# An opening in another order: the first batch's fold ahead of weight conversion, its norm on ScalarE, and weights converted by shifts and xors

## The chip, the cores and the metric

The kernel runs on one core of one Trainium2 chip. The metric is the device time of one execution in microseconds (us); lower is better. Before the change the median of 3 runs was 461.93 us (461.61 to 462.76).

A core has five engines that run their own instruction queues, each strictly in order, and wait for each other by semaphores: TensorE (PE in the profile; its weight loads are PEld), VectorE (DVE), ScalarE (ACT), GpSimd (POOL) and SyncE (SP), which here issues all the DMA transfers.

## The reference

Four batches, 1088 tokens, model width 128. Three blocks follow each other.

- Attention with a feature map instead of a softmax. For 4 heads of 32 columns, every query and key becomes the 64 products of two 8-wide projections (with S1 and S2, float64 inputs). keys give `kv = sum k_p v` and `z = sum k_p`, queries give `num / (den + 1e-6)`.
- A Fourier block: `u = x + real(fft over tokens and columns of x)`, then a layer norm `un = (u - mu) / sqrt(var + 1e-6)`, then `u + relu(un @ w_ch1) @ w_ch2` with 512 hidden columns.
- A gated block: `h = relu(x @ w_in)` with 1024 columns, halves u and v; v is normalized, mixed over tokens by a 1088 x 1088 matrix `w_spatial` with a bias, multiplied with u and projected by `w_out`.

The weights w_ch1, w_ch2, w_in and w_out reach the chip as float64 bit patterns, two 32-bit words for each number. The kernel must turn them into fp32 itself.

## The kernel before, in words

**Precision.** A large matrix product is made of three matmuls in a reduced fp32 type: high half by high half, high by low, low by high. So each operand is split: ScalarE copies it with rounding (the high half), and VectorE or GpSimd subtracts that from the original (the low half, `sub`, line 114, whose trace rows all stand under that line).

**Weight conversion.** `weight(n, k)` (line 331) takes one block of 256 columns, calls `from_f64`, lets ScalarE make the high half (line 333) and GpSimd the low half. There are ten blocks: two each of w1 and w2, four of wi (0 and 1 for u, 2 and 3 for v), two of wo. `from_f64` (line 305) splits the upper word into exponent, mantissa and sign (lines 312, 315, 316 on VectorE), shifts the exponent's range on ScalarE with two Relus (313, 314), turns the lower word into a fraction on ScalarE (311), puts mantissa and exponent together on VectorE (317, 318) and multiplies both on GpSimd (320). Its scratch tiles have two buffers each.

**Stages of one batch.** `keys(b)` and `queries(b)` make the features: three matmuls per group (line 353, `abp`), a ScalarE copy (355, two buffers `ab`), the products on VectorE (359, `pp`), then for keys 72 small matmuls (376, `kv`), for queries transposes (397, `qps`), ScalarE copies (402) and the numerator (408, `nm`), which VectorE divides into `ub[b]` (416 to 418). `fourier_seq(b)` folds the tokens and columns by the symmetry of the cosines and sines: sums and differences on VectorE (438 `eo`, 442 `fe`, 447 `l_`, 451 `lrb`) and small copies on GpSimd, then the transform's matmuls (462, `dft`). Its first pair of matmuls needs a piece of the second pass of the fold. `fourier_feat(b)` transforms the columns (491, 504) and VectorE adds the result to `ub[b]` (499, 506).

`channel(b)` (line 165) is the norm, the Fourier block's two matrix products and the v half of the gated block. Its nine token tiles come in three chunks of three. `stats` computes mean and variance of tiles on VectorE (179, 180) and 1/sigma by a ScalarE square root and four VectorE steps (`rstd`); before the change one call covers all nine tiles. For each chunk: `un`, the normalized tile, on VectorE (195); transposes (199 `t1`, 206 `t2`); the halves of the transposed tile (202 on ScalarE, `sub` on VectorE, `unl`); four hidden blocks (`ch1`, lines 214 to 216; their halves at 219 on ScalarE and 220 on VectorE, `hl`) and `ch2` (225 to 227); the sum and its halves (241 to 243), the v matmuls (254 to 256), statistics and norm of v and its halves. For batch 0 the chunk's small matmul results share two PSUM buffers.

`spatial(b)` is the token mixing (604 to 606), gate and output; its splitting of the matrix (`spatial_split`) runs on ScalarE, GpSimd and VectorE.

**Order.** The program text gives the priority: a planner walks through time with its own costs and puts on each engine's queue the ready instruction that comes first in the text; later work fills slots in which earlier work isn't ready. Three tools bend that. `issue_after(ins)` puts the instructions of a block that run on the same engine as `ins` behind it in that engine's queue (order alone, no wait). `keep_in_program_order` pins an instruction behind the one traced before it on its engine. And the hooks of `channel` run a function at a chosen chunk: `hooks[2c]` before the hidden blocks of chunk c, `hooks[2c+1]` before its v matmuls. `warm(n)` issues n matmuls of zeros that nobody reads, 11 at the start, 10 in the fold of batch 0, 20 ahead of channel(0).

The opening in the text before: loads of batch 0, tables, six weight blocks, batch 1, four weight blocks; keys(0), queries(0), weights w1, fourier_seq(0), fourier_feat(0), weights wi 2 and 3, warm(20), channel(0) (with w2 and wo converted at chunk 0, wi 0 and 1 at chunk 2), keys(1), queries(1), loads of batch 2, and the split of the first token mixing matrix. From batch 1 on, channel(b+1) is interleaved with spatial(b).

Of the kernel before, what the change touches and what calls it, by code (L numbers as in the profile page):

```python
# [7 lines left out]
F32 = mybir.dt.float32  # L8
F32R = mybir.dt.float32r
I32 = mybir.dt.int32  # L10
U32 = mybir.dt.uint32
ACTF = mybir.ActivationFunctionType
ALU = mybir.AluOpType
# [52 lines left out]
def fourier_attention_gmlp_kernel(  # L66
# [46 lines left out]
    def sub(eng, lo, x, hi):  # L113
        eng.tensor_tensor(out=lo, in0=x, in1=hi.bitcast(F32), op=ALU.subtract)  # L114
# [50 lines left out]
    def channel(b, pe, psm, tagm, nm, psc, tagc, vn, hooks=(None,) * 7):  # L165
# [9 lines left out]
        def stats(tiles):  # L175
            mv_ = pe.tile([P, len(tiles), 2], F32, tag="mv1", bufs=nb, name="mv1")
            for i, j in enumerate(tiles):
                bst = pe.tile([P, 6], F32, tag="bst", bufs=2, name="bst")
                V.bn_stats(out=bst, in_=u_[:, j, :])
                V.bn_aggr(out=mv_[:, i, :], in_=bst)  # L180
            r_ = rstd(pe, mv_, len(tiles), "l1", nb)
            for i, j in enumerate(tiles):
                mv[j], rs[j] = mv_[:, i, 0:1], r_[:, i, :]

        def hook(i):
            if hooks[i] is not None:
                hooks[i]()

        stats(range(NT))
        for c in range(3):  # L190
            c0, n, full = CH[c]
            tiles = tiles_of(c)
            un = pe.tile([P, 3, DM], F32, tag="un", bufs=nb, name="un")
            for j, i in tiles:
                marks[b, c, "un"] = V.tensor_scalar(out=un[:, i, :], in0=u_[:, j, :], scalar1=mv[j], scalar2=rs[j],
                                op0=ALU.subtract, op1=ALU.mult)
            t1 = mt("t1")
            for j, i in tiles:
                marks[b, c, "t1"] = T.transpose(out=t1[:, 128 * i:128 * i + 128], in_=un[:, i, :], identity=ident if j < 8 else psel)
            unh = pe.tile([P, 384], F32R, tag="unh", bufs=nb, name="unh")  # L200
            unl = pe.tile([P, 384], F32R, tag="unl", bufs=nb, name="unl")
            marks[b, c, "unh"] = A.copy(out=unh[:, 0:n], in_=t1[:, 0:n])
            sub(V, unl[:, 0:n], t1[:, 0:n], unh[:, 0:n])
            t2 = mt("t2")
            for j, i in tiles:
                T.transpose(out=t2[:, 128 * i:128 * i + 128], in_=u_[:, j, :], identity=ident if j < 8 else psel)
            xt = const.tile([P, 384], F32, tag="x2", bufs=3, name="xt")
            A.copy(out=xt[:, 0:n], in_=t2[:, 0:n])
            yield
            c2 = psc.tile([P, 512], F32, tag=tagc, name="c2")  # L210

# [92 lines left out]

    def from_f64(raw, n, out, fast):

        w = raw.rearrange("p (n two) -> p n two", two=2)
        lo_, hi_ = w[:, 0:n, 0], w[:, 0:n, 1]
        tl = lambda nm, dt: pre.tile([P, 256], dt, tag=nm, bufs=2, name=nm)[:, 0:n]
        x, e, s, r = tl("dx", I32), tl("dy", I32), tl("ds", I32), tl("dr", F32)  # L310
        A.activation(out=r, in_=lo_.bitcast(U32), func=ACTF.Copy, scale=2.0 ** -52)
        V.tensor_scalar(out=e, in0=hi_, scalar1=20, scalar2=0x7FF, op0=ALU.logical_shift_right, op1=ALU.bitwise_and)
        A.activation(out=e, in_=e, func=ACTF.Relu, bias=cst[:, 1:2])
        A.activation(out=e, in_=e, func=ACTF.Relu, scale=-1.0, bias=cst[:, 2:3])
        V.tensor_scalar(out=x, in0=hi_, scalar1=0xFFFFF, scalar2=0x100000, op0=ALU.bitwise_and, op1=ALU.bitwise_or)
        V.tensor_scalar(out=s, in0=hi_, scalar1=-2 ** 31, scalar2=0x7F800000, op0=ALU.bitwise_and, op1=ALU.bitwise_xor)
        V.scalar_tensor_tensor(out=r, in0=x, scalar=2.0 ** -20, in1=r, op0=ALU.mult, op1=ALU.add)
        V.scalar_tensor_tensor(out=s, in0=e, scalar=23, in1=s, op0=ALU.logical_shift_left, op1=ALU.bitwise_xor)
        out = r if out is None else out
        (V if fast else G).tensor_tensor(out=out, in0=r, in1=s.bitcast(F32), op=ALU.mult)  # L320
        return out

    wraw = {}
# [7 lines left out]
    def weight(n, k):  # L331
        w_ = from_f64(wraw.pop((n, k)), 256, None, False)
        A.copy(out=wt[n][:, k, 0, :], in_=w_)
        sub(G, wt[n][:, k, 1, :], w_, wt[n][:, k, 0, :])
# [90 lines left out]
    def fourier_seq(b):  # L425
# [10 lines left out]
        for i, op in enumerate((ALU.add, ALU.subtract)):  # L436
# [8 lines left out]
            for par in range(2):  # L445
                o2 = ALU.add if par == i else ALU.subtract
                V.tensor_tensor(out=l_[:, i, par, :, i:64], in0=ev[:, :, 0, i:64], in1=ev[:, :, 1, i:64], op=o2)
                if i == 0:
                    G.tensor_tensor(out=lz[:, :, par, 63:64], in0=eov[:, :, 0, 64:65], in1=eov[:, :, 1, 64:65], op=o2)
                rows = slice(64 * i + 32 * par, 64 * i + 32 * par + 32)  # L450
                V.tensor_tensor(out=lrb[rows, i, par, 1 - i:64 - i], in0=rs_[rows, 1:64], in1=rs_[rows, 127:64:-1], op=op)
                if i == 0:
                    G.tensor_copy(out=lrb[rows, 0, par, 0:1], in_=rs_[rows, 0:1])
                    G.tensor_copy(out=lrb[rows, 1, par, 63:64], in_=rs_[rows, 64:65])
# [86 lines left out]
    load_raw("wsh0", blocks[6:])  # L541
    keys(0)
    queries(0)
    weight("w1", 0)
    weight("w1", 1)
    fourier_seq(0)
    fourier_feat(0)
    weight("wi", 2)
    weight("wi", 3)
    warm(20)  # L550
    def convert(*part):
        def run():
            for n, k in part:
                weight(n, k)

        return run

    for _ in channel(0, pre, psy, "acc", 2, psy, "o", None, [convert(("w2", 0), ("w2", 1), ("wo", 0), ("wo", 1)), None, None, None, convert(("wi", 0), ("wi", 1)), None]):
        pass
    keys(1)  # L560
    queries(1)
    loads(2)
    with tc.issue_after(marks[0, 1, "t1"].ins):
        spatial_split(pre, 0, [G], spatial_load(const, 0, ring))
# [186 lines left out]
```

## Time and profile before

| | |
|---|---|
| median of 3 runs | 461.93 us (461.61 to 462.76) |
| the profiled execution, its own time | 462.66 us |
| its span, first to last instruction | 460.7 us |
| mean granted TensorE clock | 0.984 of full speed |
| busy: PE, DVE, ACT, POOL | 441.3, 276.4, 191.7, 68.4 us |

The rows of the later section are from the profiled execution; times in them are us from the start of its span. Busy times of TensorE are modelled ends of pipelined matmuls, so a busy engine may still run below its peak rate; its granted clock is shown beside it as a share of full speed. An idle time in a row is the engine's own idle time just before the instruction, with what ended it.

### The profile page before, as it was taken

Reading aid. Unit: us, or ns where it says so; the run is one execution under the profiler, and the core shown is the slowest. Engines: PE = TensorE matmul, PEld = TensorE weight load, DVE = VectorE, ACT = ScalarE, POOL = GpSimd, SP = SyncE. Lnnn points to the kernel's source line nnn. Section 1 sums busy time; section 2 is a strip of 40 time slices with the busy share of each in tenths; the row PEclk is TensorE's granted clock in tenths of the full one; section 3 lists DMA queues with packets and bytes.
Section 4 is the critical chain, followed back from the end, with each engine's and each line's share of the span. In section 5 each row is a group of like instructions: output and inputs, shape, how many; then the busy total and the mean of one; then the engine's idle time right before and its main releaser. Section 6 shows DMA issues by size and latency. Waiting matters only on the chain.

```text
span 460.7 us, 7484 instructions
## 1 busy us (share of the span) xinstructions
PE 441.3 (96%) x2893; PEld 405.5 (88%) x2893; DVE 276.4 (60%) x685; ACT 191.7 (42%) x448; POOL 68.4 (15%) x105
## 2 busy tenths in 40 slices
PE   8889699899999999999999999999999999999996
PEld 7766589567879789899999999999999999999995
DVE  5688988987563596789736363883645456222221
ACT  3545596365223154456524243552423335212221
POOL 2154485572110150000000000000000000000000
PEclk9979799999999999999999999999999999999999
DMA  8992132011003100000000000000000000000000
GB/s 254 359 314 97 52 92 83 0 39 34 0 1 93 38 17 1 0 1 20 14 1 0 18 0 1 18 1 14 2 0 18 0 19 1 14 1 17 1 17 16
DMA packets 13007, 19.29 MB, mean 42 GB/s; under 512 B 1446, under 2 KB 11436, under 8 KB 12844
## 3 DMA queue, kind: packets, MB, share of 16 engines
q1 hardware_dynamic: 12972, 18.82, 12.7%
q8 instruction: 23, 0.38, 0.4%
q14 instruction: 12, 0.10, 0.1%
HBM read 16.58 MB, written 2.23 MB: 41 GB/s over the span
## 4 chain that ended last, share of the span: by engine, by line
PE 77%; issue 9%; DVE 9%; ACT 3%; POOL 1%; POOLq 0%; DVEq 0%; ACTq 0%
PE ac L605 12%; PE ac L604 12%; PE ac L606 12%; PE dft L462 3%; PE v_ps L254 2%; PE v_ps L256 2%; PE c L225 2%; PE c L227 2%; PE c L226 2%; PE v_ps L255 2%; PE nm L408 2%; PE ac L612 2%; PE ac L611 1%; PE u_ps L597 1%; PE u_ps L598 1%
## 5 line engine op out<-in xcount | busy, mean ns | idle before, releaser
L606 PE MATMUL ac<-wsh,vlo 128*128 128x384 f32 (+1 forms) x384 | 126.3, 329 | 2.2 <-POOL vlo L114 2.2
L604 PE MATMUL ac<-wsh,vh 128*128 128x384 f32 (+1 forms) x384 | 126.7, 330 | 0.1
L605 PE MATMUL ac<-wsl,vh 128*128 128x384 f32 (+1 forms) x384 | 126.4, 329 | 0.0
L606 PEld LDWEIGHTS ac<-wsh,vlo 128*128 128x128 f32 x384 | 72.0, 188 | 3.3 <-POOL vlo L114 3.1
L605 PEld LDWEIGHTS ac<-wsl,vh 128*128 128x128 f32 x384 | 72.1, 188 | 1.6 <-issue 0.8
L604 PEld LDWEIGHTS ac<-wsh,vh 128*128 128x128 f32 x384 | 72.1, 188 | 1.5 <-ACT vh L270 0.4
L615 DVE TENSOR_TENSOR uh<-ac,uh 128x384 f32<-128x384 f32 (+1 forms) x48 | 25.4, 529 | 57.0 <-PE ac L612 55.2
L601 ACT ACTIVATE uh<-u_ps 128x384 f32<-128x384 f32 (+1 forms) x48 | 22.6, 471 | 48.0 <-PE u_ps L599 45.5
L114 DVE TENSOR_TENSOR gl<-uh,gh 128x384 fp32r<-128x384 f32 (+1 forms) x48 | 26.2, 548 | 12.9 <-ACT gh L616 12.7
L245 POOL CAST xh<-xh 128x64 fp32r<-128x64 f32 x4 | 2.1, 514 | 201.8 <-ACT xh L242 201.8
L359 DVE TENSOR_TENSOR pp<-ab 128x768 f32<-128x768 f32 x23 | 23.7, 1062 | 11.8 <-ACT ab L355 11.4
L261 DVE BATCH_NORM_STATS2 bst<-vn 128x6 f32<-128x512 f32 x27 | 18.6, 693 | 16.7 <-ACT vn L259 16.6
L616 ACT CAST gh<-uh 128x384 fp32r<-128x384 f32 (+1 forms) x48 | 23.5, 492 | 12.2 <-DVE uh L615 11.9
L259 ACT ACTIVATE vn<-v_ps 128x512 f32<-128x512 f32 x27 | 16.0, 598 | 19.1 <-PE v_ps L256 18.6
L241 DVE TENSOR_TENSOR xt<-c,xt 128x384 f32<-128x384 f32 (+1 forms) x12 | 6.4, 534 | 27.7 <-PE c L227 27.7
L408 PE MATMUL nm<-kvz,qp 128*128 128x66 f32 x144 | 17.4, 271 | 0.0
L408 PEld LDWEIGHTS nm<-kvz,qp 128*128 128x128 f32 x144 | 17.2, 192 | 0.1
L282 ACT CAST vh<-vn 128x1024 fp32r<-128x1024 f32 x12 | 12.6, 1047 | 10.3 <-PE ac L605 8.2
L242 ACT CAST xh<-xt 128x384 fp32r<-128x384 f32 (+1 forms) x12 | 6.0, 497 | 26.0 <-DVE xt L241 26.0
L225 PE MATMUL c<-hh,w 128*128 128x384 f32 (+1 forms) x48 | 16.6, 346 | 0.0
L597 PE MATMUL u_ps<-sxh,wi 128*128 128x384 f32 (+1 forms) x48 | 16.3, 339 | 0.3 <-ACT uh L601 0.3
L227 PE MATMUL c<-hl,w 128*128 128x384 f32 (+1 forms) x48 | 16.3, 340 | 0.0
(714 smaller groups left out, 961.6 us busy)
## 6 DMA issues: line engine op xcount, KB each, us to landing
wst<-in_wsp SPq DMA_DIRECT2D x18, 192.0 KB, 2.8
vx<-in_vt SPq DMA_DIRECT2D x12, 198.0 KB, 4.3
kt<-in_kT SPq DMA_DIRECT2D x12, 192.0 KB, 6.2
qt<-in_qT SPq DMA_DIRECT2D x12, 192.0 KB, 4.4
w2st<-in_wsp SPq DMA_DIRECT2D x9, 160.0 KB, 4.1
tr<-in_trig SPq DMA_DIRECT2D x1, 1096.0 KB
wraw<-in_w SPq DMA_DIRECT2D x4, 256.0 KB, 7.7
wraw<-in_win SPq DMA_DIRECT2D x4, 256.0 KB, 5.2
```

What stands on the lines that cost most here:

```text
L114: eng.tensor_tensor(out=lo, in0=x, in1=hi.bitcast(F32), op=ALU.subtract)
L225: mm(out=c2[:, 0:n], lhsT=wpart("w2", 0, 128 * m, 128), rhs=hh[:, 0:n], start=(m == 0), stop=False)
L227: mm(out=c2[:, 0:n], lhsT=wpart("w2", 0, 128 * m, 128), rhs=hl[:, 0:n], start=False, stop=(m == 3))
L359: (G if [b, tag[0], c] in [[3, 'k', 2]] else V).tensor_tensor(out=pp, in0=a_.unsqueeze(3).to_broadcast([P, 12, 8, 8]), in1=b_.unsqueeze(2) ...
L408: mm(out=nm[:, t, 2 * pr:2 * pr + 2, :].rearrange("p h d -> p (h d)"), lhsT=qp[:, pr, 128 * t:128 * t + 128], rhs=z[:, pr, :], start=True, ...
L597: mm(out=h_[:, 0:n], lhsT=wpart("wi", 0, 128 * m, 128), rhs=xh[:, 0:n], start=True, stop=False)
L601: A.activation(out=uh[:, 0:n], in_=h_[:, 0:n], func=ACTF.Relu)
L604: mm(out=ac[:, 0:n], lhsT=vh[:, k, ms], rhs=wsh[c][:, k, :], start=(k == 0), stop=False)
L605: mm(out=ac[:, 0:n], lhsT=vh[:, k, ms], rhs=wsl[c][:, k, :], start=False, stop=False)
L606: mm(out=ac[:, 0:n], lhsT=vl[:, k, ms], rhs=wsh[c][:, k, :], start=False, stop=False)
L615: V.tensor_tensor(out=uh[:, 0:n], in0=ac[:, 0:n], in1=uh[:, 0:n], op=ALU.mult)
L616: A.copy(out=gh[:, 0:n], in_=uh[:, 0:n])
```

## The change

- In `channel`, `stats` is called for tiles 0 to 2 alone when b is 0, and for tiles 3 to 8 behind chunk 0's transposes; for other batches it still covers nine. It computes one more small tile, minus mean times 1/sigma, and `un` becomes a ScalarE instruction with that as bias and 1/sigma as scale, for every batch.
- `from_f64` has other steps: ScalarE takes the absolute value of the upper word read as a float, a maximum and a minimum clamp it (GpSimd for weights, VectorE for the first small matrix), VectorE shifts it left and right, shifts three bits of the lower word in, and puts sign and exponent offset in by xors; the last step is on VectorE for every block.
- The VectorE instructions of w1's conversion, and of w2's (now ahead of channel(0) in place of wi 2 and 3), are queued behind the last fold instruction of batch 0. wi 2 and 3 are converted at chunk 0, wi 0 and 1 at chunk 1, wo at chunk 2.
- The VectorE instructions of keys(1) and queries(1) are queued behind `unl` of chunk 0.

```diff
             r_ = rstd(pe, mv_, len(tiles), "l1", nb)
+            m_ = pe.tile([P, len(tiles), 1], F32, tag="l1m", bufs=nb, name="m_")
+            V.scalar_tensor_tensor(out=m_, in0=mv_[:, :, 0:1], scalar=-1.0, in1=r_, op0=ALU.mult, op1=ALU.mult)
             for i, j in enumerate(tiles):
-                mv[j], rs[j] = mv_[:, i, 0:1], r_[:, i, :]
+                mv[j], rs[j] = m_[:, i, :], r_[:, i, :]
...
-        stats(range(NT))
+        stats(range(3) if b == 0 else range(NT))
...
             for j, i in tiles:
-                marks[b, c, "un"] = V.tensor_scalar(out=un[:, i, :], in0=u_[:, j, :], scalar1=mv[j], scalar2=rs[j],
-                                op0=ALU.subtract, op1=ALU.mult)
+                A.activation(out=un[:, i, :], in_=u_[:, j, :], func=ACTF.Identity, bias=mv[j], scale=rs[j])
...
-            sub(V, unl[:, 0:n], t1[:, 0:n], unh[:, 0:n])
+            marks[b, c, "unl"] = V.tensor_tensor(out=unl[:, 0:n], in0=t1[:, 0:n], in1=unh[:, 0:n].bitcast(F32), op=ALU.subtract)
...
             A.copy(out=xt[:, 0:n], in_=t2[:, 0:n])
+            if b == 0 and c == 0:
+                stats(range(3, NT))
             yield
...
-        x, e, s, r = tl("dx", I32), tl("dy", I32), tl("ds", I32), tl("dr", F32)
-        A.activation(out=r, in_=lo_.bitcast(U32), func=ACTF.Copy, scale=2.0 ** -52)
-        V.tensor_scalar(out=e, in0=hi_, scalar1=20, scalar2=0x7FF, op0=ALU.logical_shift_right, op1=ALU.bitwise_and)
-        A.activation(out=e, in_=e, func=ACTF.Relu, bias=cst[:, 1:2])
-        A.activation(out=e, in_=e, func=ACTF.Relu, scale=-1.0, bias=cst[:, 2:3])
-        V.tensor_scalar(out=x, in0=hi_, scalar1=0xFFFFF, scalar2=0x100000, op0=ALU.bitwise_and, op1=ALU.bitwise_or)
-        V.tensor_scalar(out=s, in0=hi_, scalar1=-2 ** 31, scalar2=0x7F800000, op0=ALU.bitwise_and, op1=ALU.bitwise_xor)
-        V.scalar_tensor_tensor(out=r, in0=x, scalar=2.0 ** -20, in1=r, op0=ALU.mult, op1=ALU.add)
-        V.scalar_tensor_tensor(out=s, in0=e, scalar=23, in1=s, op0=ALU.logical_shift_left, op1=ALU.bitwise_xor)
+        a, s, r = tl("dx", I32), tl("ds", I32), tl("dr", F32)
+        A.activation(out=a.bitcast(F32), in_=hi_.bitcast(F32), func=ACTF.Abs)
+        (V if fast else G).tensor_scalar(out=a.bitcast(F32), in0=a.bitcast(F32), scalar1=2.0 ** -15, scalar2=1.875 * 2.0 ** 16,
+                                         op0=ALU.max, op1=ALU.min)
+        V.tensor_scalar(out=s, in0=hi_, scalar1=-2 ** 31, scalar2=0x40000000, op0=ALU.bitwise_and, op1=ALU.bitwise_xor)
+        V.tensor_scalar(out=a, in0=a, scalar1=4, scalar2=1, op0=ALU.logical_shift_left, op1=ALU.logical_shift_right)
+        V.scalar_tensor_tensor(out=s, in0=lo_, scalar=29, in1=s, op0=ALU.logical_shift_right, op1=ALU.bitwise_xor)
         out = r if out is None else out
-        (V if fast else G).tensor_tensor(out=out, in0=r, in1=s.bitcast(F32), op=ALU.mult)
+        V.tensor_tensor(out=out.bitcast(I32), in0=a, in1=s, op=ALU.bitwise_xor)
...
-                V.tensor_tensor(out=lrb[rows, i, par, 1 - i:64 - i], in0=rs_[rows, 1:64], in1=rs_[rows, 127:64:-1], op=op)
+                marks[b, "fold"] = V.tensor_tensor(out=lrb[rows, i, par, 1 - i:64 - i], in0=rs_[rows, 1:64],
+                                                   in1=rs_[rows, 127:64:-1], op=op)
...
-    weight("w1", 0)
-    weight("w1", 1)
     fourier_seq(0)
+    with tc.issue_after(marks[0, "fold"].ins):
+        weight("w1", 0)
+        weight("w1", 1)
     fourier_feat(0)
-    weight("wi", 2)
-    weight("wi", 3)
+    with tc.issue_after(marks[0, "fold"].ins):
+        weight("w2", 0)
+        weight("w2", 1)
     warm(20)
...
-    for _ in channel(0, ..., [convert(("w2", 0), ("w2", 1), ("wo", 0), ("wo", 1)), None, None, None, convert(("wi", 0), ("wi", 1)), None]):
+    for _ in channel(0, ..., [convert(("wi", 2), ("wi", 3)), None, convert(("wi", 0), ("wi", 1)), None, convert(("wo", 0), ("wo", 1)), None]):
         pass
-    keys(1)
-    queries(1)
+    with tc.issue_after(marks[0, 0, "unl"].ins):
+        keys(1)
+        queries(1)
     loads(2)
```

## Rows read from the trace of the kernel before

**Rows 1.** Stretches: PE, PEld, DVE, ACT, POOL busy us; TensorE clock; DMA share, GB/s.
```profile
20.00:30.00 10.00, 7.34 (x88) 6.63 (x90) 9.90 (x25) 4.83 (x13) 3.85 (x10) 0.99 0.98 314
30.00:40.00 10.00, 10.00 (x66) 5.84 (x64) 7.37 (x21) 4.95 (x14) 6.47 (x7) 0.67 0.76 249
...
50.00:58.00 8.00, 7.12 (x26) 6.08 (x26) 7.22 (x18) 4.46 (x11) 2.78 (x4) 0.57 0.03 10
...
80.00:110.00 30.00, 26.17 (x200) 19.53 (x200) 28.23 (x53) 14.65 (x33) 17.48 (x22) 1.00 0.10 27
...
200.00:400.00 200.00, 200.00 (x1196) 193.98 (x1195) 116.71 (x293) 83.35 (x185) 2.21 (x6) 1.00 0.02 8
```

**Rows 2.** Timeline of TensorE, 28 to 53 us: start, length, line, operation [idle before].
```profile
28.06 3.23 PE L376 MATMUL kv<-vx,pp 128*64 128x33 f32 x72 [2.05 <-DVE pp L359]
...
31.63 1.18 PE L462 MATMUL dft<-tr,l__380 128*64 128x274 f32 x2
...
41.60 4.84 PE L519 MATMUL wp<-a 128*128 128x512 f32 x20
...
50.15 0.42 PE L199 MATMUL t<-prm,un 128*128 128x128 f32 x1 [3.31 <-DVE un L195]
...
52.37 0.69 PE L214 MATMUL h__605<-unh,w 128*128 128x384 f32 x1 [0.74 <-ACT unh L202]
```

**Rows 3.** Timeline of VectorE, 20 to 32 us.
```profile
20.39 0.28 DVE L316 TENSOR_SCALAR ds<-wraw 128x256 int32<-128x256 int32 x1
...
22.20 0.69 DVE L438 TENSOR_TENSOR eo<-ub 128x512 f32<-128x512 f32 x1
...
26.24 0.29 DVE L312 TENSOR_SCALAR dy<-wraw 128x256 int32<-128x256 int32 x1
...
27.05 3.56 DVE L359 TENSOR_TENSOR pp<-ab 128x768 f32<-128x768 f32 x4
...
31.46 0.49 DVE L447 TENSOR_TENSOR l__380<-fe 128x126 f32<-128x126 f32 x2
```

**Rows 4.** Groups by line and form, 0 to 120 us: busy, mean ns | idle before.
```profile
L313 ACT ACTIVATE dy<-dy,cst 128x256 int32<-128x256 int32 x10 | 4.9, 504 | 4.3 <-DVE dy L312 4.3
...
L195 DVE TENSOR_SCALAR un<-ub,mv,r 128x128 f32<-128x128 f32 x9 | 3.3, 434 | 0.0
...
L179 DVE BATCH_NORM_STATS2 bst<-ub 128x6 f32<-128x128 f32 x9 | 2.1, 268 | 0.0
...
L313 ACT ACTIVATE dy<-dy,cst 128x64 int32<-128x64 int32 x1 | 0.3, 348 | 0.0
```

**Rows 5.** The same view: conversion and products.
```profile
L359 DVE TENSOR_TENSOR pp<-ab 128x768 f32<-128x768 f32 x18 | 18.1, 1047 | 5.8 <-ACT ab L355 5.5 <-PE kv L376 0.3
...
L320 POOL TENSOR_TENSOR dr<-dr,ds 128x256 f32<-128x256 f32 x10 | 7.9, 797 | 7.4 <-DVE ds L318 7.3
...
L318 DVE SCALAR_TENSOR_TENSOR ds<-dy,ds 128x256 int32<-128x256 int32 x10 | 5.4, 544 | 1.6 <-ACT dy L314 1.5
...
L312 DVE TENSOR_SCALAR dy<-wraw 128x256 int32<-128x256 int32 x10 | 4.7, 474 | 0.1
L317 DVE SCALAR_TENSOR_TENSOR dr<-dx,dr 128x256 f32<-128x256 int32 x10 | 4.7, 472 | 1.1 <-ACT dr L311 1.1
...
L316 DVE TENSOR_SCALAR ds<-wraw 128x256 int32<-128x256 int32 x10 | 3.6, 358 | 0.0
...
L315 DVE TENSOR_SCALAR dx<-wraw 128x256 int32<-128x256 int32 x10 | 2.8, 276 | 0.0
```

**Rows 6.** Stretch from 52 to 80 us, VectorE alone: busy, clock, DMA.
```profile
52.00:80.00 28.00, 24.19 (x57) 0.91 0.26 72
```

**Rows 7.** Line 451 by its operations: min/median/max ns, first and last start.
```profile
L451 DVE TENSOR_TENSOR lrb<-rs__1229 x4: 203/218/1198, 84.8 to 91.9; 32x63 f32<-32x63 f32 x4
```

**Rows 8.** GpSimd's timeline from 85 us.
```profile
85.01 3.89 POOL L114 TENSOR_TENSOR vlo<-v,vh 128x512 fp32r<-128x512 f32 x3
```

**Rows 9.** Groups, 0 to 120 us: the activation tables' load.
```profile
L511 ACT ACT_TABLE_LOAD x1 | 1.3, 1283 | 0.7 <-PEq L737 0.7
```

More of the change, by code (lines that the diff above doesn't have):

```diff
@@ L556, in convert @@
         return run
-    for _ in channel(0, pre, psy, "acc", 2, psy, "o", None, [convert(("w2", 0), ("w2", 1), ("wo", 0), ("wo", 1)), None, None, None, convert(("wi", 0), ("wi", 1)), None]):
+    for _ in channel(0, pre, psy, "acc", 2, psy, "o", None, [convert(("wi", 2), ("wi", 3)), None, convert(("wi", 0), ("wi", 1)), None, convert(("wo", 0), ("wo", 1)), None]):
         pass
-    keys(1)
-    queries(1)
+    with tc.issue_after(marks[0, 0, "unl"].ins):
+        keys(1)
+        queries(1)
     loads(2)
```

## The prediction

> **What bounds the kernel now.** I read the table of stretches first. From 110 us on TensorE has hardly a gap: 200 of 200 us are busy between 200 and 400, at the full clock [rows 1]. Its work there does not change, so whatever the opening saves reaches the end unless another engine takes it back on the way. The loss lies before 110. TensorE was granted a mean clock of 0.67 between 30 and 40 us and 0.57 between 50 and 58, so parts of these stretches ran at 1.2 GHz; between 80 and 110 it is busy 26.17 of 30 us. In the same table VectorE is nearly full: 9.90 of 10 us (20 to 30) and 28.23 of 30 (80 to 110).
>
> Next TensorE's own timeline, for what it waits on [rows 2]. At 28.06 it has waited 2.05 us for a product of batch 1. It then enters the Fourier matmuls (31.63) with the low clock. After the filler of 20 matmuls (41.60 to 46.4) and four small ones it waits 3.31 us for the first normalized tile, and the first weight matmuls (52.37) fall into the second stretch with a low clock. Both times the clock fell behind a gap of 2 to 3 us.
>
> Last VectorE's timeline for the cause [rows 3]. Attention of batch 0 ends at about 20.4, but the fold (lines 438 to 451), which the Fourier matmuls need, is cut up: conversion from 20.39 to 22.20, again at 26.24, four products of batch 1 at 27.05, and only at 31.46 the last half of the fold.
>
> What can be got back at most: the two gaps, 2.05 + 3.31 = 5.4; the clock between 30 and 40, 10 x (1 - 0.67) = 3.3; between 50 and 58, 8 x (1 - 0.57) = 3.4; in all 12.1, say 12.2 with the 0.1 lost between 20 and 30. The filler's 4.84 us stays, since nothing removes it.
>
> **The change, part by part.**
>
> *Order around the fold.* The VectorE instructions of keys and queries of batch 1 go behind the low half of chunk 0, and those of w1 and w2 behind the fold. From VectorE's rows this takes 1.81 us (20.39 to 22.20), 0.81 (26.24 to 27.05) and some 3.5 (the four products from 27.05) out of the fold's way, with about 0.5 of smaller pieces: 6.6. The Fourier matmuls then start near 25 instead of 31.63. TensorE has batch 1's feature matmuls to fill until then, up to five groups of six before buffers stop it, so I expect no gap and the full clock. From 31.63 to the filler's start behind the second transform (41.60) is 10.0 us [rows 2]. Less the 3.3 of clock, and an estimated 1 of batch 1's transposes and features that lie in between, it is about 5.7; the filler starts near 31 instead of 41.6.
>
> *Statistics of three tiles instead of nine.* Six of nine statistics, 0.27 us each plus an aggregate [rows 4], leave the path to the first normalized tile. Three statistics, the square root and four small VectorE steps (the new one, minus mean times 1/sigma, among them) take about 3 us, then three ScalarE instructions. The filler, 4.84 us, now lasts longer than this chain, so the 3.31 gap goes and the filler itself is late next: t1 at about 36 instead of 50.15, and the clock stays up for chunk 0.
>
> *Normalizing on ScalarE.* VectorE pays 0.434 us per tile in the opening [rows 4]. ScalarE's form has a per-partition bias and scale. The nearest row is ScalarE with a bias on 256 elements, 0.504 [rows 4]; on 64 it took 0.348; these are the bounds, and I take 0.45. Three of them cost between 0.3 less and 0.2 more than on VectorE, under the filler's cover; uncovered, that goes onto the path. For batches 1 to 3, 27 tiles x 0.45 = 12 us move to a ScalarE that is half idle; TensorE is full there, so I count 0, at worst 0.3 per chunk, 2.7.
>
> The Trainium skill, "ScalarE: Activation LUTs", Rules for kernel authors, says to put additions and multiplications on VectorE, which speaks against this move; by its section What ACT_TABLE_LOAD costs, an estimate for 128 elements with two pointer operands is 0.48 us. By that three tiles would take 0.14 us more than VectorE's 0.434 each, against 0.05 by my value.
>
> *Conversion.* Per block of 256 columns VectorE had 0.474 + 0.276 + 0.358 + 0.472 + 0.544 = 2.12 us in five instructions [rows 5]; it now has four: a sign step (0.36 as line 316), a double shift (0.28 to 0.47, as lines 315 and 312), and two two-input steps (0.47 to 0.54 each). I take 1.7, so ten blocks save 4 us, bounds 2.5 to 5. ScalarE loses two instructions of about 0.5 each (line 313, and 314 like it) [rows 4]. GpSimd's product, 0.797 [rows 5], becomes a clamp of one input; no row shows it, bounds 0.4 (half) and 1.3 (a subtraction of 512 elements [rows 8]); I take 0.8, no change. VectorE's double shift now waits for ScalarE and then GpSimd; behind it queue whatever VectorE instructions follow, statistics above all. The scratch has two buffers, so block three's first step on ScalarE waits for block one's last on VectorE, with ScalarE's evictions behind it. With w1 begun at 25 and 1.7 to 2 us per block, w1 is there near 29 and w2 near 33, before t1.
>
> *What is late next.* VectorE's deferred work. From 52 to 80 it was busy 24.19 of 28 us, so 3.8 were free [rows 6]. Into the like stretch of the new kernel come four of batch 1's products (4 x 1.05 = 4.2 [rows 5]), two more blocks of conversion than before less their saving (about 1.3), half of the six late statistics with their aggregates (an estimated 1.3), and three tiles' normalizing leaves (3 x 0.434 = 1.3): 5.5 more, 1.7 beyond what was free. Instructions do not pack perfectly, so I charge 2.5. TensorE's displaced work (batch 1's 72 matmuls, 3.23 us [rows 2]) lies in the gaps that this leaves. Batch 1's products also free the input buffers on which SP's queue waits; those loads serve stretches beyond 110, so nothing.
>
> Sum: 12.2 - 2.5 = 9.7 us. The profiled execution took 462.66 (span 460.7 and 1.96 around it), which gives 453.0; it stands 0.73 above the median of the runs, so the median forecast is 452.2.
>
> **Rivals.** *More.* The lighter VectorE pays all its debt and also closes half of the 3.83 us that TensorE idles between 80 and 110: 12.2 + 1.9 = 14.1, or 447.8. For it: no VectorE work is added, 4 us of conversion and 3.3 of normalizing go. Against: VectorE is at 28.23 of 30 in that stretch.
>
> *Half.* GpSimd's clamps no longer wait for VectorE (line 320 waited for line 318), so they start while the fold runs. One form of line 451 took 0.203 us at best and 1.198 at worst [rows 7], in a stretch in which GpSimd ran three subtractions of 1.3 us [rows 8]. Two or three such collisions move the Fourier matmuls by 1.5; batch 1's features run out, a gap opens, and the clock falls as it did after the 2.05 gap. Then 1.5 + 3.3 are lost on top of the 2.5: gain 4.9, or 457.0. The Trainium skill, "SBUF — State Buffer", Who interferes with whom, says that a VectorE instruction with two SBUF inputs and a GpSimd one that reads SBUF block each other for the whole instruction; the trace's 1.198 would agree with that. By it each fold step (all have two inputs) could wait a whole clamp.
>
> *Slower.* Chunks 0 to 2 of batch 0 starve behind the queue on VectorE: products of batch 1 and conversion stand before the low halves, TensorE gets gaps of 2 us and more as in [rows 2], and the clock falls through the stretch. Of 28 x 0.91 = 25.5 us of full-rate TensorE time there [rows 6], half at 1.2 GHz costs 13 more: 9.7 - 13 = -3.3, or 465.2. It decides once such gaps come more than twice there. Against: by 36 us the fold, w1 and w2 have left VectorE's queue, and batch 1's products are not needed by chunks 0 to 2.
>
> *Not what it says.* If Abs or Identity needed other tables than the square root, each return would cost a load of 1.283 us [rows 9]; ten blocks would eat the gain, about 462. One load in the trace serves square root, Relu and copies, which makes it unlikely. Or the planner, which places instructions by its own times, fills the freed slots so that t1 hardly moves: also about 462.
>
> **How the numbers follow.** Forecast 0.50 (452.2, own range 449.5 to 455), more 0.17 (447.8), half 0.20 (457.0, from 455 to 460), no change 0.05, slower 0.08. A difference under 0.3% (1.4 us) can't be told from none. So faster 0.87, same 0.05, slower 0.08. The range from 446.5 to 460.0 leaves out no change, slower, and the edges of the two neighbours.
>
> **What would show it.** Right: the Fourier matmuls near 25 at the full clock; t1 near 36 with no gap before it; a granted clock near 1 from 20 to 60; the first main accumulation (line 604) near 70 instead of 79. The 2.5 us shows as TensorE idle on VectorE's low halves or on late weights between 36 and 70. Wrong: a low clock in the Fourier matmuls (half), repeated gaps with a fallen clock in chunks 0 to 2 (slower), or more table loads.

## The result and the profile after

The change makes the kernel slower: 467.79 us (463.80 to 469.43, 12 runs) against 462.17 (461.60 to 463.33, 12 runs), a ratio of 1.0100 with a 95% interval of 1.0072 to 1.0129 (the ratio is close to that of the means, 466.87 and 462.22; the medians lie 5.6 us apart). Forecast were 452.2 us and a range of 446.5 to 460.0.

One execution of the changed kernel was profiled with the result (464.61 us, span 462.6); the first experiment added a second one (469.21, span 467.3). Stretches of the first, columns as in [rows 1]:

```profile
20.00:30.00 10.00, 8.30 (x48) 5.45 (x48) 7.42 (x24) 2.05 (x6) 4.62 (x10) 1.00 1.00 331
30.00:40.00 10.00, 7.14 (x36) 5.17 (x36) 9.57 (x39) 4.05 (x12) 6.74 (x9) 1.00 0.03 9
...
50.00:58.00 8.00, 5.73 (x52) 4.59 (x49) 6.91 (x11) 5.19 (x13) 6.44 (x8) 1.00 0.19 52
...
80.00:110.00 30.00, 25.85 (x219) 19.86 (x219) 24.85 (x48) 13.72 (x32) 16.06 (x20) 1.00 0.10 28
```

Some of the same stretches of the second, of the same program:

```profile
20.00:30.00 10.00, 8.48 (x44) 6.00 (x44) 7.90 (x26) 2.05 (x6) 3.24 (x9) 0.83 0.99 316
...
50.00:58.00 8.00, 5.30 (x39) 4.50 (x40) 6.80 (x11) 5.05 (x13) 5.54 (x6) 0.84 0.30 79
...
80.00:110.00 30.00, 26.35 (x179) 20.81 (x178) 24.19 (x50) 14.73 (x33) 17.30 (x21) 0.94 0.07 21
...
170.00:200.00 30.00, 27.70 (x147) 25.62 (x145) 19.53 (x44) 17.20 (x41) 4.74 (x5) 0.94 0.00 1
```

The reader is to see two things. TensorE's clock, low in two stretches of [rows 1], is full in the first execution and falls in the second. And even at the full clock TensorE is idle more: 2.27 us of 8 between 50 and 58, against 0.88 in [rows 1], and 2.86 between 30 and 40, against none.

The same columns from 20 to 200 us, of the kernel before, then of the changed one in its first and its second execution; 180 less the first number is TensorE's idle time, 12.4, 17.9 and 16.2 us:

```profile
20.00:200.00 180.00, 167.63 (x1185) 140.09 (x1186) 137.29 (x343) 87.89 (x214) 63.03 (x86) 0.96 0.20 60
```

```profile
20.00:200.00 180.00, 162.10 (x1178) 136.18 (x1178) 130.83 (x319) 86.05 (x214) 63.63 (x84) 1.00 0.20 60
```

```profile
20.00:200.00 180.00, 163.76 (x1153) 138.82 (x1153) 128.05 (x312) 82.95 (x206) 63.06 (x84) 0.95 0.20 61
```

TensorE's timeline after, in the first execution (start, length, line, operation, idle time before), beside [rows 2]. `tb` is ScalarE's copy of the transform's first half, `xl` the low half of a chunk's sum:

```profile
25.04 0.88 PE L465 MATMUL dft<-tr,l__346 128*64 128x274 f32 x5 [1.26 <-DVE l__346 L449]
...
31.80 1.13 PE L494 MATMUL ups<-dd,tb 128*128 128x256 f32 x4 [1.81 <-ACT tb L487]
...
33.64 4.85 PE L522 MATMUL wp<-a 128*128 128x512 f32 x20
39.31 1.10 PE L200 MATMUL t<-prm,un 128*128 128x128 f32 x3 [0.82 <-ACT un L197]
...
41.60 0.42 PE L217 MATMUL h__559<-unh,w 128*128 128x384 f32 x1
...
49.62 0.89 PE L378 MATMUL kv<-vx,pp 128*64 128x33 f32 x24
...
53.96 0.50 PE L259 MATMUL v_ps<-wi,xl 128*128 128x512 f32 x1 [2.27 <-DVE xl L114]
...
90.69 0.45 PE L610 MATMUL ac<-wsh,vh 128*128 128x384 f32 x1 [1.85 <-ACT vh L273]
...
174.04 0.33 PE L200 MATMUL t<-prm,un 128*128 128x128 f32 x1 [2.26 <-ACT un L197]
```

The opening does what was forecast: Fourier matmuls at 25.04, filler at 33.64, first weight matmul at 41.60 instead of 52.37. That is 10.8 us earlier, but some 7 of them are work put off: matmuls of batch 1 (features, `kv`, `qps`) took TensorE 8.8 us between 20 us and the first weight matmul in the kernel before and 1.4 in the changed one, where `kv` begins at 49.62 instead of 28.06. The lead that is left is given back in waits. VectorE's timeline tells where the one at 53.96 comes from; line 319 is the double shift behind GpSimd's clamp (line 316):

```profile
29.44 0.85 DVE L319 TENSOR_SCALAR dx<-dx 128x256 int32<-128x256 int32 x1 [1.66 <-POOL dx L316]
...
50.53 0.47 DVE L319 TENSOR_SCALAR dx<-dx 128x256 int32<-128x256 int32 x1 [0.65 <-POOL dx L316]
51.56 1.08 DVE L319 TENSOR_SCALAR dx<-dx 128x256 int32<-128x256 int32 x1 [0.55 <-POOL dx L316]
52.56 1.34 DVE L114 TENSOR_TENSOR xl<-xt,xh 128x384 fp32r<-128x384 f32 x1
```

`xl`, for which TensorE waits, stands in the queue behind two conversions of wo, which nobody needs yet and which themselves wait for GpSimd. The two waits are 1.2 us of the delay. The second shift and `xl` also took 1.08 and 1.34 us; with a short clamp (e9 below) the two shifts together take 0.70 and `xl` 0.55. They ran while GpSimd was at the first subtractions of the spatial split:

```profile
51.49 1.99 POOL L114 TENSOR_TENSOR wsl<-wst,wsh 128x384 fp32r<-128x384 f32 x2
```

Whether GpSimd made them longer was not tested here; e17 below shows it for other steps. ScalarE's queue stalls likewise: its cast at 31.05 had waited 2.44 us for a conversion, with the copy of `tb` behind it:

```profile
31.05 0.41 ACT L335 CAST w<-dr 128x256 fp32r<-128x256 f32 x1 [2.44 <-DVE dr L322]
```

### The profile page after: what moved, and what is told of

It reads as the page before. It is cut to its first block, busy times and chain, and to the rows that moved or that the text cites. A ratio compares the mean times of both kernels' runs of the same rounds, so it can differ in the third digit from the quotient of the medians.

```text
span 462.6 us, 7454 instructions
## 1 busy us (share of the span) xinstructions
PE 437.5 (95%) x2893; PEld 403.4 (87%) x2893; DVE 267.4 (58%) x647; ACT 195.0 (42%) x463; POOL 71.1 (15%) x105
## 4 chain that ended last, share of the span: by engine, by line
PE 72%; issue 10%; DVE 10%; POOL 4%; ACT 3%; DMA 1%; POOLq 0%; ACTq 0%; DVEq 0%
PE ac L610 12%; PE ac L612 12%; PE ac L611 12%; PE v_ps L259 2%; PE v_ps L257 2%; PE dft L465 2%; PE abp L355 2%; PE v_ps L258 2%; PE c L230 2%; PE c L228 2%; PE ac L618 2%; PE ac L617 1%; PE u_ps L603 1%; PE c L229 1%; PE u_ps L604 1%
## 5 line engine op out<-in xcount | busy, mean ns | idle before, releaser
L259 PE MATMUL v_ps<-wi,xl 128*128 128x512 f32 x36 | 15.2, 421 | 3.2 <-DVE xl L114 3.2
L603 PE MATMUL u_ps<-sxh,wi 128*128 128x384 f32 (+1 forms) x48 | 16.2, 338 | 0.0
```

Source lines behind the costliest of these rows:

```text
L259: mm(out=h_, lhsT=xl[:, cs], rhs=wt["wi"][:, 2:4, 0, :], start=False, stop=True)
L603: mm(out=h_[:, 0:n], lhsT=wpart("wi", 0, 128 * m, 128), rhs=xh[:, 0:n], start=True, stop=False)
```

## Experiments

The ratio of each run is to the kernel before on the same chip; its interval is 95%.

**The changed kernel again, and without the edge on batch 1.** e1 is unedited. e3:

```diff
-    with tc.issue_after(marks[0, 0, "unl"].ins):
-        keys(1)
-        queries(1)
+    keys(1)
+    queries(1)
```

> The changed kernel once more, unedited, for a second trace: its timed runs lie between 463.8 and 469.4 us and the one profiled run of it (464.6 us) had TensorE at its upper level throughout. All theories: a median of 465 to 469. If the spread is the clock, a profiled run near 468 shows the granted clock below 1.00 in some stretch, and some 3 to 4 us of doubled matmul time there; if it is not the clock, the granted clock is 1.00 and the added time is idle time of TensorE.

> The changed kernel without the edge that holds keys and queries of batch 1 until the first low half of chunk 0 is made; all else stays. Theory 1 (conversion chain stalls the queues): 465 to 469, since the conversion is the same and VectorE gets the feature products back beside it. Theory 2 (borrowed lead): 459 to 462, the first matmul of h near 47 to 50 us instead of 41.6, but batch 1's transform matmuls back from 95.8 to 91 us or before.

e1: 467.18 us, 1.0091 (1.0062 to 1.0121). e3: 468.12, 1.0101 (1.0068 to 1.0134); its queues came out in the same order, so the edge holds nothing back and e3 is one more repeat. Of the 12 runs with the result, three had a mean granted clock of 0.997 to 1.000 and took 463.8 to 464.6; seven had 0.979 to 0.983 and took 467.8 to 469.4. The spread goes with the clock. Where it falls, e1's TensorE (the second execution) shows:

```profile
21.92 3.88 PE L522 MATMUL wp<-a 128*128 128x512 f32 x10
...
35.02 6.40 PE L522 MATMUL wp<-a 128*128 128x512 f32 x20
...
55.34 0.66 PE L259 MATMUL v_ps<-wi,xl 128*128 128x512 f32 x1 [2.24 <-DVE xl L114]
```

The same fillers took 2.54 and 4.85 us at the full clock; each of these three stretches at 1.2 GHz lies behind a wait, 1.54 us for the piece of `ub` behind which the first fillers run, 1.81 for `tb`, 2.24 for `xl`. The first execution had the same waits (1.55, 1.81 and 2.27) at the full clock.

**The clamp.** e2 puts the old `from_f64` into the changed kernel. e4 and e9 edit one line of the new one, e4 with all columns and VectorE, e9 with GpSimd and 32 columns (the other 224 stay unclamped):

```diff
-        (V if fast else G).tensor_scalar(out=a.bitcast(F32), in0=a.bitcast(F32), ...
+        V.tensor_scalar(out=a.bitcast(F32), in0=a.bitcast(F32), ...                                     (e4)
+        (V if fast else G).tensor_scalar(out=a[:, 0:32].bitcast(F32), in0=a[:, 0:32].bitcast(F32), ...  (e9)
```

> The changed kernel with the old weight conversion (two Relu and one scaled copy on ScalarE, four steps on VectorE, the product on GpSimd) in place of the new one; order of work, the norm on ScalarE and the split statistics stay. Theory 1 (the new conversion's chain, ScalarE to GpSimd to VectorE to ScalarE, stalls the in-order queues between 26 and 56 us): 458 to 461 us, the first VectorE waits of 1.66 and 0.65 us for the clamp gone. Theory 2 (the lead is borrowed: keys and queries of batch 1 are kept out of TensorE's gaps and have to be done later): no gain, 466 to 470, since VectorE then has some 0.4 us more per block.

> The changed kernel with the clamp of every weight block on VectorE instead of GpSimd (the form that the small block already uses); all else stays. It adds ten clamps of 0.2 to 0.5 us to VectorE and takes ten of 1.05 to 1.23 us from GpSimd. Theory 1 (it is the hop over GpSimd that stalls VectorE and, behind it, ScalarE): 460 to 464. Theory 2 (borrowed lead): 466 to 470, as VectorE has 2 to 5 us more to do.

> The changed kernel (467.2 to 467.8) with GpSimd's clamp cut to the first 32 of 256 columns of a block (the other columns go unclamped, so values near zero there are not caught); TensorE's, ScalarE's and SyncE's queues stay instruction for instruction, VectorE's differ in two swaps of neighbours. Theory 1 (it is the 1.05 to 1.23 us that the clamp holds the block, with VectorE's and ScalarE's queues behind it): clamp near 0.4 us, TensorE's waits for xl (2.3) and tb (1.8) under 1 us, 461 to 465. Theory 2 (it is the place that the other instructions were given in the queues, which the clamp on VectorE changed as well): 466 to 469.

e2: 470.75, 1.0161 (1.0121 to 1.0202). e4: 459.93, 0.9925 (0.9900 to 0.9950). e9: 463.01, 1.0010 (0.9995 to 1.0025). Groups of line 316 on GpSimd: the changed kernel, then e9; then VectorE's in e4 (busy, mean ns, idle before):

```profile
L316 POOL TENSOR_SCALAR dx<-dx 128x256 f32<-128x256 f32 x10 | 10.9, 1098 | 14.4 <-ACT dx L315 14.4
```

```profile
L316 POOL TENSOR_SCALAR dx<-dx 128x32 f32<-128x32 f32 x10 | 3.5, 352 | 14.8 <-ACT dx L315 14.8
```

```profile
L316 DVE TENSOR_SCALAR dx<-dx 128x256 f32<-128x256 f32 x10 | 2.8, 279 | 0.4 <-ACT dx L315 0.4
```

e9 keeps the queues, but for two shifts on VectorE, and shortens the clamp by 0.75 us; that alone returns 0.8 to 0.9% (3.7 to 4.2 us), and `tb` and `xl` cost TensorE 0.3 and 1.0 us instead of 2.1 and 3.2. VectorE's steps ahead of the first `xl`, and the columns from 20 to 200 us, in e9:

```profile
48.79 0.70 DVE L319 TENSOR_SCALAR dx<-dx 128x256 int32<-128x256 int32 x2
49.41 0.55 DVE L114 TENSOR_TENSOR xl<-xt,xh 128x384 fp32r<-128x384 f32 x1
```

```profile
20.00:200.00 180.00, 168.42 (x1181) 141.07 (x1182) 129.27 (x323) 86.43 (x215) 57.73 (x84) 0.95 0.20 61
```

Its idle time, 11.6 us, is best held against e1's 16.2, which has the same clock of 0.95: 4.7 us less. So the clamp's length on GpSimd, with what comes late by it, is worth the loss against the kernel before; taking it away doesn't bring the gain that was forecast. e4 ends at the lower edge of its first theory's range, 3 us below e9, but its queues have another order than e9's, so those 3 us have no single cause here. e2 is ten above the first theory's range, just above the second's: with the old conversion the new order loses still more, so the new conversion is not what made the order a loss.

**One part alone on the kernel before.** e5: the new `from_f64`. e6: the same with e4's line. e7: the norm on ScalarE for all batches. e12: for batch 0 alone.

```diff
+                if b == 0:      (e12; e7 has the next line for every batch)
+                    A.activation(out=un[:, i, :], in_=u_[:, j, :], func=ACTF.Identity, bias=mv[j], scale=rs[j])
...
```

> The kernel before with the new conversion alone, clamp on GpSimd; the order of the program, the norm and the statistics stay as before. Theory 1 (the hop over GpSimd costs wherever the conversion stands): slower than the same with the clamp on VectorE (run with it) by 5 to 8 us, as in the changed kernel (467.2 against 459.9). Theory 2 (the hop costs only where conversions lie between the transform and the first norm, as the new order has it): within 2 us of it. Against the kernel before (463.3): 460 to 466 by theory 1, 457 to 461 by theory 2.

> The kernel before with the new conversion alone and every clamp on VectorE. Theory 1 (the reorder itself is a loss, which the changed kernel with the old conversion shows at 470.8 against 463.3, and a conversion without GpSimd is a gain by itself): 454 to 458, below the changed kernel with the clamp on VectorE (459.9). Theory 2 (the reorder is worth its 3 to 10 us once the conversion doesn't stall it): 461 to 464, above it.

> The kernel before with the first norm on ScalarE alone, with the small extra step that it needs on VectorE in every batch; all else as before. If the norm on ScalarE is part of the loss (ScalarE's in-order queue holds it behind conversion casts, and in later batches behind other evictions): 465 to 468. If it is neutral: 462 to 464. If it takes work from the engine that paces the opening: 459 to 462.

> The kernel before with the first norm on ScalarE for batch 0 alone. With it for all batches it took 467.2 against 462.4. Theory 1 (1.3 us of that is the later batches' wait at the first transpose, the rest the opening): 465 to 466.5. Theory 2 (the opening doesn't lose by it): 461.5 to 463.

e5: 461.90, 0.9991 (0.9972 to 1.0010). e6: 462.06, 0.9997 (0.9984 to 1.0010). e7: 467.23, 1.0102 (1.0060 to 1.0144). e12: 466.86, 1.0093 (1.0075 to 1.0110). In the old order it doesn't matter which engine clamps: the same clamp that costs 4 us in the new order costs nothing here, as theories 2 of e5 and e6 have it (e5's time itself lies 0.9 above the range given there; and the planner ordered the queues of e5 and e6 differently, so this compares two plans). Moving the norm to ScalarE is a loss here already for batch 0, and e7 and e12, whose queues differ by little but the later norms, are equal. But little of the loss lies at that norm: the wait of 3.31 in [rows 2] became 3.90 in e12. More of it lies at batch 2's first transpose, whose norm is on VectorE as before: 2.32 us, against 0.92 before the change. Over 20 to 200 us e12's TensorE is idle for 15.3 us (12.4 before), and its clock is 0.95 (0.96 before):

```profile
50.58 0.47 PE L205 MATMUL t<-prm,un 128*128 128x128 f32 x1 [3.90 <-ACT un L199]
...
175.75 0.30 PE L205 MATMUL t<-prm,un 128*128 128x128 f32 x1 [2.32 <-DVE un L201]
```

```profile
20.00:200.00 180.00, 164.72 (x1159) 138.48 (x1160) 129.09 (x321) 88.44 (x216) 64.61 (x86) 0.95 0.19 60
```

The edit also moved other instructions in the queues, so what the norm's engine costs by itself stays open. The first theory of e12, 0.4 below the result, falls with its reason: without the later norms the time is the same, and the long wait at batch 2 is still there.

**From e4 on.** e8: the norm back on VectorE for all batches. e10: on ScalarE for batch 0 alone. e11: e10 with w2 and all later blocks ordered behind the last addition of batch 0's transform.

```diff
-    with tc.issue_after(marks[0, "fold"].ins):
+    with tc.issue_after(marks[0, "ub"].ins):      (e11: w2, and each later convert)
```

> The changed kernel with every clamp on VectorE (459.9 by itself) and the first norm back on VectorE, without the extra small step. If the norm on ScalarE is part of the loss: 455 to 458. If neutral: 459 to 461. If it was a gain: 462 to 465.

> The changed kernel with every clamp on VectorE (459.9), the first norm on ScalarE for batch 0 alone and on VectorE, as before the change, for batches 1 to 3. In every trace with the later norms on ScalarE the first transpose of batch 2 waits 2.2 us near 170 us, with them on VectorE 0.9 us [before]. Theory 1 (that wait is the price of the later norms): 458.3 to 459.3. Theory 2 (any such edit gives the queues another order, and that weighs more): outside 457 to 461.

> As the run before it (clamps on VectorE, norm of batch 0 on ScalarE), and the conversion of w2 and of all later blocks ordered behind the last of the three additions that end batch 0's transform. In the trace with clamps on VectorE those additions begin at 34.9 us, some 2 us after their operand, behind conversion steps. Theory 1 (conversions ahead of the additions are on the path): the additions begin near 33, the first matmul of h near 40.5 in place of 42.5, 456 to 458. Theory 2 (what is put off comes back as waits for w2 and wi in chunk 0): no faster than the run before it, 459 to 463.

e8: 475.37, 1.0291 (1.0270 to 1.0312). e10: 458.13, 0.9901 (0.9884 to 0.9917), the best version with e18. e11: 475.81, 1.0283 (1.0258 to 1.0308). e10 ends 0.2 below the range of its first theory, but not for its reason: the wait of 2.16 us at batch 2's first transpose in e4 only fell to 1.70, and the 0.9 that the expectation gives to norms on VectorE is found in the kernel before alone (e5 and e6 wait 1.82, e12 2.32). The clock from 140 to 200 us, 0.98 and 0.96 in e4, was full. The intervals of e4 and e10 touch, so the step between them is not certain. e8 and e11 lie ten and more above every theory. Both traces lose the time in the same places; TensorE's timeline of e11:

```profile
65.44 0.50 PE L264 MATMUL v_ps<-wi,xl 128*128 128x512 f32 x1 [3.63 <-DVE xl L114]
...
101.78 0.65 PE L470 MATMUL dft<-tr,l__1199 128*64 128x274 f32 x2 [2.92 <-DVE l__1199 L454]
107.24 1.63 PE L470 MATMUL dft<-tr,l__1199 128*64 128x274 f32 x5 [4.27 <-DVE l__1199 L454]
```

Batch 1's fold comes 17 us later than in e10 (106.89 against 90.14). Both edits changed the order of all the queues. Why it came out so was not tested; it stays open, and e8 therefore doesn't tell what the norm's engine is worth.

**What sets the end.** In the traces up to here the end mostly followed batch 1's last fold on VectorE by 366 to 369 us (e7 and e12: 372 and 374). e13 and e14 cut VectorE's work before and behind that fold, on the changed kernel; e15 and e16 start from e10:

```diff
-                V.bn_stats(out=bst, in_=v_)
+                V.bn_stats(out=bst, in_=v_[:, 0:128] if b == 0 else v_)      (e13; e14: b == 1)
...
-    warm(20)
+    warm(40)      (e15; e16 has keys(1) and queries(1) ahead of channel(0) instead)
```

> The changed kernel with the nine batch statistics of v in batch 0 taken over 128 of 512 columns (0.69 us each becomes some 0.26), which leaves the statistic short; it frees some 3.9 us of VectorE between 53 and 90 us and nothing of TensorE's work. Theory 1 (VectorE up to the last fold of batch 1 paces the opening, the end follows that fold 367 to 369 us later): fold 3 to 4 us earlier, 463 to 464.5 against 467.2 to 467.8. Theory 2 (TensorE's own waits and clock around batch 0's chunks set it): 466 to 468.5.

> The control: the same cut of the statistics in batch 1 in place of batch 0, that is after the last fold of batch 1, where TensorE has the spatial matmuls of batch 0 to go on with. Theory 1: no change, 466.5 to 468.5. If VectorE's work counts wherever it stands: 463 to 464.5.

> The kernel with clamps on VectorE and the norm of batch 0 alone on ScalarE (458.1), with 40 filler matmuls in place of 20 ahead of the first transpose: the opening of batch 0 loses up to 4.9 us of its lead (20 by 0.24). Theory 1 (VectorE up to batch 1's fold paces): 457.5 to 460. Theory 2 (the lead of batch 0 on TensorE is what counts): 462 to 463.5.

> The same kernel (458.1) with keys and queries of batch 1 put ahead of batch 0's channel part in the program, so that they go first where both are ready. Theory 1: batch 1's last fold ends before 90.6 us and the end comes 367 to 369 us later, 454 to 457.5, even if the first matmul of h is later than 44. Theory 2 (the lead of batch 0 counts): 459 to 464, since the norm and the splits of chunk 0 wait behind the feature products.

e13: 465.88, 1.0074 (1.0051 to 1.0097). e14: 468.30, 1.0103 (1.0072 to 1.0135). e15: 464.75, 1.0062 (1.0039 to 1.0085). e16: 464.32, 1.0043 (1.0027 to 1.0059). The fold theory falls: in e16 the fold's last step (line 454 there) starts 12 us earlier than in e10 (78.26 against 90.14), and the kernel is 6 us slower, 0.3 above its second theory; chunks 0 to 2 now wait (TensorE from 58 to 80):

```profile
58.00:80.00 22.00, 16.29 (x70) 11.19 (x68) 21.91 (x44) 14.26 (x32) 15.76 (x20) 0.92 0.25 74
```

The lead of batch 0 is worth at least its full length: 20 more fillers, 4.5 us of TensorE (9.36 against 4.83), cost 1.6%, some 7 us and 1.3 more than the second theory allows. The two profiled executions are 5.4 us apart (spans of 462.9 and 457.4), 0.9 of it more idle time. Behind the fillers TensorE waits 1.87 us and has a low clock; e10 has as much low clock at other places (0.66 from 20 to 30 us, 0.92 from 58 to 80):

```profile
50.00:58.00 8.00, 7.48 (x62) 6.50 (x63) 6.04 (x8) 3.54 (x10) 3.95 (x3) 0.57 0.32 95
```

e13 lies between its two theories: of the 3.9 us some 1 to 2 came back, if any (its interval touches those of e1 and e14); e14 gave nothing.

**GpSimd beside VectorE**, from e10. e17 orders the split of the spatial matrix's first chunk behind `marks[0, 2]`; e18 gives every second of its subtractions to VectorE:

```diff
-    with tc.issue_after(marks[0, 1, "t1"].ins):
-        spatial_split(pre, 0, [G], spatial_load(const, 0, ring))
+    with tc.issue_after(marks[0, 2].ins):                                   (e17)
+        spatial_split(pre, 0, (V, G), spatial_load(const, 0, ring))         (e18)
```

> The kernel with clamps on VectorE and the norm of batch 0 alone on ScalarE (458.1), with the split of the spatial matrix's first chunk ordered behind the end of batch 0's last channel chunk in place of the first transpose of its second one: GpSimd's eight subtractions leave the stretch from 46 to 66 us, in which VectorE's feature products took 1.50 to 1.77 us against 0.95 alone. Theory 1 (GpSimd beside VectorE lengthens VectorE's steps, and these hold TensorE): products near 0.95 there, TensorE's idle time between 58 and 80 us below the 2.2 us of before the edit, 455.5 to 458. Theory 2 (the spatial matmuls are needed to fill TensorE from 74 us on, and now come later): 459 to 465.

> The same kernel (458.1) with every second of these eight subtractions on VectorE (0.55 us each, 2.2 us in all) in place of GpSimd (1.2 us each beside VectorE). Theory 1 (GpSimd beside VectorE is the price): 456 to 458.5, since VectorE gains back what it takes on. Theory 2 (VectorE's own work in the opening is the price): 459 to 461.

e17: 462.13, 0.9981 (0.9964 to 0.9998), as its second theory has it. e18: 458.31, 0.9888 (0.9871 to 0.9906), within its first theory and the same as e10. Feature products on VectorE in e10, then in e17:

```profile
52.79 1.77 DVE L366 TENSOR_TENSOR pp<-ab 128x768 f32<-128x768 f32 x1
56.62 1.77 DVE L366 TENSOR_TENSOR pp<-ab 128x768 f32<-128x768 f32 x1
```

```profile
51.28 0.95 DVE L366 TENSOR_TENSOR pp<-ab 128x768 f32<-128x768 f32 x1
57.98 0.95 DVE L366 TENSOR_TENSOR pp<-ab 128x768 f32<-128x768 f32 x1
```

The collision is real: between 50 and 58 us GpSimd is busy for 6.72 us in e10 and not at all in e17, and six products take 6.25 us instead of 8.61. Yet TensorE then has 26 spatial matmuls instead of 36 from 58 to 90 us, its idle time from 58 to 80 us rises from 2.2 to 4.6, and its clock from 80 to 90 is 0.66 instead of 1.00: 4 us lost. The Trainium skill, "SBUF — State Buffer", Who interferes with whom, says that VectorE's instructions with two SBUF inputs and GpSimd's that read SBUF exclude each other; the products' 0.95 and 1.77 agree.

## Why the prediction was wrong

*The miss in two terms.* A gain of 9.7 us was forecast and 5.6 were lost. The 9.7 are 2.9 less idle time of TensorE and 6.8 less low clock. e1's trace, at the usual clock, has 3.9 more idle time than the kernel before (16.2 against 12.4) and 1.7 more low clock (some 8.5 us against 6.8, each stretch times 1 less its granted share). That is 6.8 and 8.5 us off the forecast, 15.3 in all. The sum fits the medians; e1's own execution took about 1 us more.

*Confirmed.* The Fourier matmuls at 25.04 (forecast 25; a wait of 1.26 stood before them, where none was expected), w2's last cast at 32.66 (33), the filler at 33.64 (31), the first transpose at 39.31 with a wait of 0.82 (36, no wait), the first main accumulation at 73.24 (70). The last three are some 3 us late, of which 1.81 is the wait for `tb`. One reason given was wrong: by e3 the edge on keys and queries of batch 1 moves nothing; the planner had put them there anyway.

*The step that failed: the conversion's cost of "0.8, no change" for the clamp.* It took 1.10 us on average, inside the stated bounds, but it was priced as GpSimd's time, which is free. The text named the wait of line 319 and what queues behind it, and put no number on it. e9 prices it: about 4 us, and 4.7 of the 6.8 us of idle time. The weights w1 and w2 were on time; what came late stood behind a conversion.

*What is late next, 2.5 us.* TensorE's idle time was to fall from 12.4 to 9.5 (less 5.4, plus 2.5); it was 17.9, and 16.2 in e1. The free 3.8 us of VectorE [rows 6] were no measure: its queue stands in order, and 1.2 us of waits in it, with the longer steps behind them, stopped TensorE for 2.27. With the clamp short (e9, 11.6) or on VectorE (e10, 9.8) it comes near 9.5.

*The step that failed beside it: the clock, 6.8 us.* The ceiling took the full clock as won for good. It was in the profiled execution; most others had a low clock in new places. e1 shows them: in the first fillers, behind the wait of 1.81 for `tb`, the wait of 2.24 for `xl`, in 80 to 110 and at batch 2's first transpose. The two profiled executions of one program lie 4.7 us of span apart. A short clamp doesn't settle this: e9 has 0.95 from 20 to 200 us like e1. Why the clock falls in one execution and not in another, behind the same waits, stays open.

*The norm on ScalarE.* Its length was near: three take 1.26 us, 0.42 each, against 0.45. The cover was short: statistics and small steps took 3.6 us (35.12 to 38.76) instead of about 3. VectorE has five small steps there, not four, and ran conversion and late statistics between them. So the first transpose waits 0.82 behind the filler:

```profile
38.76 1.26 ACT L197 ACTIVATE un<-ub,m__488,r 128x128 f32<-128x128 f32 x3 [1.15 <-DVE m__488 L183]
```

The later norms were counted 0, at worst 2.7. At batch 2's first transpose TensorE waits 2.26 us instead of 0.92 before the change, but e12 waits 2.32 there with those norms on VectorE, so the wait can't be put down to their engine. e10 without them is 1.8 us faster than e4, if the step is real; e12 without them is no faster than e7.

*The rivals.* "Slower" had its place and mechanism nearly right (chunks behind VectorE's queue, gaps of 2 us, falling clock) and its 465.2 is nearest to the result. The number is luck: half of the time from 52 to 80 us at 1.2 GHz was to cost 13 us, and e1 loses some 1.7 to the clock there (0.84 from 50 to 58 us, 0.98 from 58 to 80). It got 0.08 because the argument against it looked at w1 and w2 alone, and the xl that stalled stood behind wo. "Half" had the clamp colliding with the fold; the fold was untouched (line 453's steps took 0.21 to 0.22 us). "Not what it says": no further table load shows.

*Left over.* e10 and e18 keep 4 to 5 of the 9.7 us. At e10, idle time is near the forecast, but the clock is still 0.66 between 20 and 30 and 0.92 between 58 and 80 us. And one sum does not close: the changed kernel's first execution lost 17.9 us to idle time and none to the clock, the kernel before 12.4 and 6.8, that is 1.3 more, yet it ended 1.9 earlier. Some 3 us of busy TensorE time before 200 us came on top, and no run tells why.

## What to carry to other kernels

Price a hop to another engine by the queue that waits behind it, not by that engine's free time; test it by shortening the hopped step at an unchanged order. Here most edits to the program changed the order of every queue (e8 and e11 ended 15 and 18 us above the runs they started from), so compare the queues before pricing an edit. Work that nobody needs yet belongs behind work that TensorE waits for, above all if it has to wait itself. Forecast a recovered clock as a chance: while waits of 1.5 us and more stay, as here, it may fall behind those instead.

## What the runs showed of the hardware

- A one-input clamp (maximum, then minimum) of 128x256 on GpSimd takes 1.06 to 1.23 us, longer than the two-input product of the same size that it replaced (0.797 [rows 5]), and four times VectorE's 0.279. Between 32 and 256 columns it grows by (1.065 - 0.317) / 224 = 3.3 ns per column (medians). The Trainium skill, "GPSIMD Engine Reference", Engine selection, calls one-input steps on GpSimd roughly line-rate; this measurement differs and decides.
- With the same queues and nearly the same waits, one program kept TensorE's full clock through its opening in one execution and in another had a granted clock of 0.83 from 20 to 40 us, 0.84 from 50 to 58, 0.94 from 80 to 110 and 0.94 from 170 to 200.
